# Where the last two "values" steps of a chunk put their sums, and another order of steps, in an mLSTM and GELU kernel

## The chip, the cores and the metric

One core of one Trainium2 chip runs the whole program. The metric is the time of one execution on the device, in microseconds (us); lower is better. The kernel before takes 438.91 us, the median of 3 runs from 438.79 to 439.17.

## The reference

The inputs are q, k, v and an output gate for 4 batches, 8 heads, 768 positions and 40 dimensions, an input gate and a forget gate for every position, and two weight matrices (320 x 2048 and 2048 x 320). An mLSTM cell runs over the positions; its output, seen as 3072 tokens of 320 numbers, goes through a two-layer network with exact GELU:

```
for t in range(S):
    m_new = np.maximum(f[t] + m, i[t])
    f_stab, i_stab = np.exp(f[t] + m - m_new), np.exp(i[t] - m_new)
    C = f_stab * C + i_stab * outer(v[t], k[t]);  n = f_stab * n + i_stab * k[t];  m = m_new
    y[t] = sigmoid(o[t]) * (C @ q[t]) / np.maximum(abs(n @ q[t]), 1)
h = y @ w_in                                   # 3072 x 2048
out = (0.5 * h * (1 + erf(h / sqrt(2)))) @ w_out
```

## The kernel before

**Tiles and stages.** The positions are cut into six chunks of 128. Within a chunk the recurrence is replaced by matrix products: a matrix of scores between the 128 positions (query times key), weighted by exponentials of the gates, times the values, plus the contribution of the state carried from the chunks before. A *cell* c (class `Cell`) does this for chunk c, batch by batch (b is 0 to 3). A *chunk* c (class `Chunk`) is the two-layer network on the 512 tokens that cell c made. Cell c+1 is computed while the network of chunk c runs, and its instructions are threaded between those of the network.

The network's products are made in three passes with each operand split into a high part and a rest, all on TensorE (PE in the profile). The *up* product of a chunk has four quarters. `up` (steps U0 to U3, line 966) makes a quarter's sums over the first 256 of the 320 features, in four banks of PSUM, the accumulator memory; `up_rest` (u0 to u3, line 977) adds the last 64. `gelu` (g0 to g15, lines 984 to 987) reads a bank: ScalarE (ACT) applies GELU and takes the high part, VectorE (DVE) makes the rest and the low part. `down` (d0 to d15, line 991) multiplies each of these 16 pieces with its rows of w_out and adds into four accumulators `po`, one bank each. A bank has 512 columns and `po` uses 320; the next 164 columns of each bank are called `beside`.

**The steps of a cell** inside chunks (cells 2 to 5): M masks the weight matrix W on GpSimd (POOL, line 474), W takes its exponentials (ACT, line 500), K and Q turn keys and queries (DVE, line 512), D weighs the values (POOL, line 539), S0 and S2 make the scores of two batches (PE line 568, DVE line 574), C0 and C2 read the state for two batches (`read_two`, PE line 621), h0 and h2 update it (`update_two`, PE line 632, DVE lines 639 and 647, POOL line 643), V0 to V3 multiply scores and values (`later_values`, PE line 674, DVE line 678), Y normalises and gates (`finish`, DVE lines 685 to 690), t copies the last 64 features twice (line 699), X transposes the result on PE (`turn_y`, line 708) and takes its high part on ACT (line 718), and R makes the other two parts (`split_x`, DVE lines 727 and 728). B loads the next W, J and O load the next keys, values and gates, L loads blocks of turned keys and queries, and + copies keys and queries in DRAM for later blocks, all on SyncE's DMA queue (SP). E0 to E3 copy a finished chunk's `po` out. In V0 and V1 the sums go into `beside`, in V2 and V3 into a bank of their own, which they can get only when no quarter of `up` holds it; DVE then adds the sums to `far`, the part from the state.

**Front.** Before chunk 1, cells 0 and 1 and the network of chunk 0 run in the order of the string `FRONT`. There K and J convert pieces of the weights that DMA brought as 64-bit numbers (ACT lines 404 and 405, DVE lines 416 and 419; each J fetches a later piece), A and U are quarters of `up` in plain fp32 (lines 818 and 824), u, i and f are others in split form, F are the 16 rows of `down` (line 888), z splits a piece of GELU's result (lines 873 to 875) for the last six F, and a and b make the parts of w_out (lines 935 and 943).

**What sets the order.** Every engine works through its own instructions in the order in which they are issued and waits on semaphores. The order is written out by hand in the strings: `FRONT`, then `SECOND` for chunk 1, `LATER` for chunks 2 to 4 and `LAST` for chunk 5, which has no cell beside it. A letter is a step and the number its argument. A number above 3 after M or W means the cell after the next. Inside a chunk the four banks that are not `po` are two pools of two, `side[0]` and `side[1]`; the pairs of banks of `up`, S, C and X take turns in them. Some SBUF tiles are shared by their tag in the same way: `sig` has two buffers, `o_sb` two, and a new use waits until the last reader of the old one is done.

Of the kernel before, what the change touches and what calls it, by code (L numbers as in the profile page):

```python
# [9 lines left out]
F32 = mybir.dt.float32  # L10
# [13 lines left out]


FRONT = """
    O0 L0 k1 P0 E L1 L2 t0 P1 k7 K w0 g0 N s0 w1 O1 O3 D k4 t1 P2 w2 c0 v0 J y0 Q s1 L3 O2 K d w3 q t2 L4 P3 v1
    g1 c1 J y1 s2 K x0 t3 x1 v2 g2 O4 J B4 g3 c2 y2 s3 B5 K x2 K L5 J T0 K v3 A y3 M1 x3 c3 G0 M0 H O7 O6 O5 J
    J i5 u0 L6 u1 K W0 J W1 I4 A K S0 T1 C0 J i6 V0 i7 u2 G2 K U M2 L7 S1 J G1 K U i8 W2 J i9 C1 T2 K
    M3 f2 S2 V1 Y0 T3 J Y1 C2 e W3 K K K J S3 J C3 f3 K X0 J K R0 J K J V2 K Y2 J J K  # L30
    K V3 X1 J K r F J K (0 )0 F J K F K J F X2 G3 F J K F Y3 R1 J K F p + + + + J F J a10,2 b10,2 z10 a12 b12 F X3 z11 F a13,3 b13,3 z12 F z13 [1 F B8 z14 F B9 R2 z15 F R3 B10 B11 F a8 b8 a9 b9 F"""
CELL = "MWGVYXRKQDCSht"

HI_AT = {3: ("w_out3", 0), 8: ("w_out3", 2), 4: ("w_out0", 0), 5: ("w_out0", 1), 6: ("w_out2", 0), 7: ("w_out2", 1), 9: ("f0", 0)}
# [1 line left out]
for at, first, key in ((HI_AT, 10, "h0"), (LO_AT, 10, "h1"), (HI_AT, 13, "b0"), (LO_AT, 13, "b1"), (HI_AT, 0, "b2"), (LO_AT, 0, "b3")):  # L36
    at.update((first + i, (key, i)) for i in range(3))
LATER = """
 U0 u0 E0 E1 E2 E3 K1 Q1 L2 D0 D1 C0 h0 M2 M3 g0 g1 g2 g3 +
 U1 u1 g4 d0 g5 d1 g6 d2 g7 S0 d3 K2 Q2 L3 W2 W3 G0 G1 G2 G3 +  # L40
 U2 V0 V1 u2 g8 d4 g9 K3 Q3 B4 B5 J0 J1 d5 g10 d6 g11 S2 L4 d7
 U3 u3 + M4 M5 Y0 Y1 D2 D3 K4 W4 W5 g12 t0 d8 g13 t1 d9 g14 X0 X1 R0 d10 g15 R1 C2 h2 O0 O1 d11 V2 V3 Y2 t2 B6 J2 d12 Y3 t3 Q4 L5 B7 d13 X2 X3 R2 d14 R3 d15 + O2 O3"""

SECOND = """
 U0 u0 j2 o0 o1 K1 Q1 L2 M0 M1 D0 D1 W0 W1 a0,3 b0,3 a3 b3 a4,2 b4,2 a6,2 b6,2 C0 h0 M2 M3 g0 g1 g2 g3 o2 o3 + +
 U1 u1 Z Z Z g4 d0 g5 d1 g6 d2 g7 S0 d3 K2 Q2 L3 W2 W3 G0 G1 G2 G3 Z Z +
 U2 V0 V1 u2 + g8 d4 g9 K3 Q3 B4 B5 J0 J1 d5 g10 d6 g11 S2 L4 d7
 U3 u3 + M4 M5 Y0 Y1 D2 D3 K4 W4 W5 g12 t0 d8 g13 t1 d9 g14 X0 X1 R0 d10 g15 R1 C2 h2 O0 O1 d11 V2 V3 Y2 t2 B6 J2 d12 Y3 t3 Q4 L5 B7 d13 X2 X3 R2 d14 R3 d15 + O2 O3"""

LAST = """  # L50
 U0 u0 E0 E1 E2 E3 g0 g1 g2 g3 U1 u1 g4 d0 g5 d1 g6 d2 g7 d3 
# [5 lines left out]
def kernel(  # L57
# [28 lines left out]
    TG = B * L
# [45 lines left out]
    vb = [const.tile([P, H, D1], F32, name=f"vb{n}", tag=f"vb{n}") for n in range(NQ)]  # L132
# [250 lines left out]
    bits, sig, pow2 = {}, {}, {}  # L383
# [51 lines left out]
    def per_head(t, c, b):  # L435
        return t[:, c, b * H:(b + 1) * H].unsqueeze(2)
# [21 lines left out]
    class Cell:  # L458
# [153 lines left out]
        def read_two(self, b0):  # L612

            c, two_b = self.c, (b0, b0 + 1)
            banks = self.banks = [self.side[1][0].tile([P, H + NP, D1], F32, name="pf", tag=self.side[1][1]) for _ in range(2)]
            for i, b in enumerate(two_b):
                qT = self.qT[b]
                for p in range(NP):
                    for r in halves:
                        for hip in range(2):  # L620
                            nc.tensor.matmul(banks[hip][r, NP * i + p, :], qT[halves[hip], p, r],  # L621
                                             state[b][halves[hip], p, 0:D1], start=True, stop=True)

        def update_two(self, b0):

            c, two_b, banks = self.c, (b0, b0 + 1), self.banks
            if c + 1 < NCH:
                for i, b in enumerate(two_b):
                    vw = self.vw.pop(b)
                    for p in range(NP):  # L630
                        for hip in range(2):
                            nc.tensor.matmul(banks[i][used[hip], H + p, :], k_later[turn_of(c * B + b)][:, 2 * p + hip, :],  # L632
                                             vw[:, 2 * p + hip, :], start=True, stop=True)
            add = []
            for i, b in enumerate(two_b):
                self.far[b] = fars[0].tile([P, H, D1], F32, name="far", tag="hs", bufs=2)
                by_hip = lambda t, hip: t.rearrange("p (m two) d -> p m two d", two=2)[:, :, hip, :]
                for hip in range(2):
                    nc.vector.tensor_tensor(out=by_hip(self.far[b], hip), in0=banks[hip][:, NP * i:NP * i + NP, :],  # L639
                                            in1=by_hip(per_head(gT, c - 1, b), hip).to_broadcast([P, NP, D1]), op=OP.mult)  # L640
# [19 lines left out]

        def later_values(self, b):

            n, hs = self.c * B + b, self.far.pop(b)
            Pm = W.pop(n)
            by_hip = lambda t: [t.rearrange("p (m two) d -> p m two d", two=2)[:, :, hip, :] for hip in range(2)]
            if b < 2:
                ph = beside[2 * b:2 * b + 2]
            else:
                whole = self.side[0][0].tile([P, H, D1], F32, name="ph", tag=self.side[0][1])
                ph = by_hip(whole)  # L670
            for hip in range(2):
                for p in range(NP):
                    for r in quarters:
                        nc.tensor.matmul(ph[hip][r, p, :], Pm[:, 2 * p + hip, r], vb[turn_of(n)][:, 2 * p + hip, :], start=b > 1,  # L674
                                         stop=True, skip_group_check=b < 2)
            self.hs[b] = hs
            for to, x in zip(by_hip(hs), ph) if b < 2 else ((hs, whole),):
                nc.vector.tensor_tensor(out=to, in0=x, in1=to, op=OP.add)

        def finish(self, b):  # L680
            n, hs = self.c * B + b, self.hs.pop(b)
# [18 lines left out]

        def turn_y(self, b):
            n, t = self.c * B + b, slice(b * L, (b + 1) * L)
            pool, tag = self.side[b // 2] if self.c > 1 else (ps_tr, "tr") if self.c > 0 else (ps_mm, "b")
            px = pool.tile([P, NX + 1, L], F32, name="px", tag=tag)
            unread(px[:, 0, :])
            for k in range(NX + 1):
                y = ob[n % NLD][:, k * P:(k + 1) * P] if k < NX else self.rest.get(b, y_rest).rearrange("p two r -> p (two r)")
                nc.tensor.transpose(px[:, k, :], y, ident)  # L708
            self.turned.append(b)
            if self.c < 2 and len(self.finished) > len(self.turned):  # L710
                self.twice(b + 1)
            if self.c == 0:
                nc.scalar.copy(out=first_x[:, :, t], in_=px)
                return
            self.px[b] = px
            if "x" not in parts:
                parts["x"] = raw.tile([P, NX + 1, TG], F32R, name="x_hi", tag="x", bufs=1)
            nc.scalar.activation(out=in_place(parts["x"], b), in_=by_set(px), func=AF.Copy, scale=PART)
            if self.c == 1 and b < 2:
                load(n + NLD, 1, 3)  # L720
# [12 lines left out]
    parts, fars, w_hi, w_lo, beside = {}, [], {}, {}, []  # L733
# [304 lines left out]
    def first_blocks():  # L1038
# [3 lines left out]
        for r in (32, 96):  # L1042
# [65 lines left out]
```

## Time and profile before

| | |
|---|---|
| median of 3 runs | 438.91 us |
| the profiled execution | 438.46 us |
| its span, first to last instruction | 436.7 us |
| PE busy | 427.3 us, 98% of the span |
| DVE, ACT, POOL busy | 296.0, 277.3 and 48.8 us |
| granted TensorE clock | 1.0 all through |

The profiled execution is 0.45 us under the median of the runs, and 1.8 us of it lie outside the span. The timeline view lists instructions of an engine in order of time, runs of equal ones merged: start, length, engine, line, what is written from what, the shape and, in brackets, idle time before it and what ended that. A run's length reaches to the modelled end of its last instruction, so lengths overlap the next row's start a little. The view of the chain that ended last gives pieces in order of time with start and length, without overlap, and the waits view gives who waited for whom, with total, count and longest.

### The profile page before, as it was taken

To read this page: it belongs to the slowest core of one execution; us is meant where nothing else is said; L and a number is where in the kernel's file an instruction comes from. 1 tells how busy PE (TensorE), PEld (TensorE's weight loads), DVE (VectorE), ACT (ScalarE), POOL (GpSimd) and SP (SyncE) were. 2 spreads that over 40 slices of the span, in tenths; PEclk is the share of its full clock that TensorE was granted. 3 is DMA by queue.
4 is the path that set the end of the run, shared out by engine and by line. 5 is a ranking of instruction groups with operands and counts; after the bars stand their busy time and mean duration, and the time that the engine had idled before them with its cause. 6 is when DMAs were issued, how large, how long until landed. Compare 5 with 4: busy or idle time off the path is not lost.

```text
span 436.7 us, 13291 instructions
## 1 busy us (share of the span) xinstructions
PE 427.3 (98%) x5472; PEld 374.6 (86%) x5472; DVE 296.0 (68%) x680; ACT 277.3 (63%) x595; POOL 48.8 (11%) x77
## 2 busy tenths in 40 slices
PE   8989999999999999999999999999999999999996
PEld 7777888877988899988899988899988889979986
DVE  8797687797888697747597747597746586533330
ACT  4989999856889985228785229785247715243441
POOL 3001030000430041030041030040010000000000
PEclk9999999999999999999999999999999999999999
DMA  7999994577791592662492653571561400010001
GB/s 151 220 214 243 233 256 87 138 211 179 229 154 56 106 176 60 115 179 50 84 187 42 123 158 60 117 134 32 110 156 17 62 2 2 22 42 2 1 2 60
DMA packets 162268, 48.83 MB, mean 112 GB/s; under 512 B 147776, under 2 KB 155232, under 8 KB 162208
## 3 DMA queue, kind: packets, MB, share of 16 engines
q1 hardware_dynamic: 161888, 47.65, 50.1%
q8 instruction: 43, 0.70, 0.6%
q10 hardware_dynamic: 320, 0.33, 0.2%
q14 instruction: 17, 0.14, 0.1%
HBM read 43.84 MB, written 9.37 MB: 122 GB/s over the span
## 4 chain that ended last, share of the span: by engine, by line
PE 73%; DVE 2%; ACT 2%; DMA 1%; issue 1%; ACTq 0%
PE po L991 31%; PE pu L966 24%; PE pu L977 7%; PE ps L568 3%; PE pf L621 2%; PE ph L674 1%; PE po L888 1%; PE po L674 1%; PE px L708 1%; DMA bits<-in_moe_w_out_dram 1%; PE pf L632 1%; DVE pow L416 1%; DVE w_out L419 0%; ACT w_out_part L935 0%; ACT g_part L873 0%
## 5 line engine op out<-in xcount | busy, mean ns | idle before, releaser
L991 PE MATMUL po<-w_out_part,g_parts 128*128 128x320 f32 x960 | 140.7, 303 | 0.0
L991 PEld LDWEIGHTS po<-w_out_part,g_parts 128*128 128x128 f32 x960 | 131.6, 189 | 5.9 <-issue 4.6
L986 DVE TENSOR_TENSOR g_parts<-g_whole,g_parts 128x512 fp32r<-128x512 f32 x80 | 57.0, 713 | 58.1 <-ACT g_parts L985 56.0
L984 ACT ACTIVATE g_whole<-pu 128x512 f32<-128x512 f32 x80 | 47.1, 589 | 74.2 <-PE pu L977 63.7
L985 ACT ACTIVATE g_parts<-g_whole 128x512 fp32r<-128x512 f32 x80 | 50.5, 631 | 8.3 <-PE po L991 5.1
L474 POOL TENSOR_SCALAR_AFFINE_SELECT W<-W 128x1024 f32<-128x1024 f32 (+2 forms) x20 | 21.7, 1088 | 189.2 <-DMA W<-M_d 154.4
L500 ACT ACTIVATE W<-W,aT 128x128 f32<-128x128 f32 x128 | 38.8, 389 | 0.3
L987 DVE CAST g_parts<-g_whole 128x512 fp32r<-128x512 f32 x80 | 36.2, 453 | 0.0
L699 ACT COPY far<-ob 128x128 f32<-128x128 f32 x16 | 4.6, 290 | 32.9 <-DVE ob L690 32.9
L966 PE MATMUL pu<-x_hi,w_in_hi 128*128 128x512 f32 x80 | 24.2, 384 | 0.0
L966 PE MATMUL pu<-x_hi,hi_first 128*128 128x512 f32 x80 | 24.0, 381 | 0.1
L966 PE MATMUL pu<-x_rest,hi_first 128*128 128x512 f32 x80 | 23.8, 379 | 0.0
L966 PE MATMUL pu<-x_rest,w_in_hi 128*128 128x512 f32 x80 | 23.8, 379 | 0.0
L966 PE MATMUL pu<-x_low,w_in_lo 128*128 128x512 f32 x80 | 23.8, 379 | 0.0
L966 PE MATMUL pu<-x_low,w_in 128*128 128x512 f32 x80 | 23.8, 379 | 0.0
L888 PE MATMUL po<-w_out,g 128*128 128x320 f32 x80 | 22.0, 432 | 0.0
L404 ACT ACTIVATE sig<-bits 128x320 f32<-128x320 f32 (+1 forms) x26 | 15.2, 586 | 10.4 <-issue 6.1
L574 DVE TENSOR_TENSOR W<-ps,W 128x256 f32<-128x256 f32 (+1 forms) x48 | 17.7, 414 | 4.2 <-PE ps L568 3.2
L888 PEld LDWEIGHTS po<-w_out,g 128*128 128x128 f32 x80 | 15.0, 190 | 5.9
L639 DVE TENSOR_TENSOR far<-pf,gT 128x164 f32<-128x164 f32 x32 | 8.4, 319 | 16.1 <-PE pf L632 11.7
L416 DVE SCALAR_TENSOR_TENSOR pow<-sig,pow 128x320 uint32<-128x320 uint32 (+1 forms) x26 | 15.4, 592 | 4.3 <-ACT pow L405 4.3
L1015 ACT ACTIVATE o_sb<-po 128x320 f32<-128x320 f32 x20 | 7.5, 443 | 16.7 <-PE po L991 16.7
(196 smaller groups left out, 778.9 us busy)
## 6 DMA issues: line engine op xcount, KB each, us to landing
W<-M_d SPq DMA_DIRECT2D x16, 512.0 KB, 6.5
bits<-in_moe_w_in_dram SPq DMA_DIRECT2D x20, 256.0 KB, 4.2
bits<-in_moe_w_out_dram SPq DMA_DIRECT2D x16, 320.0 KB, 4.6
blocks<-kq_d SPq DMA_DIRECT2D x32, 128.0 KB, 3.5
ob<-in_o_gate_dram SPq DMA_DIRECT2D x24, 160.0 KB, 4.1
out_dram<-o_sb SPq DMA_DIRECT2D x36, 80.0 KB, 2.0
wide<-M_d SPq DMA_DIRECT2D x4, 512.0 KB, 4.8
kq_d<-in_k_dram SPq DMA_DIRECT2D x6, 320.0 KB, 4.6
```

Of the source, the lines that this page charges most:

```text
L416: nc.vector.scalar_tensor_tensor(out=p, in0=s, scalar=3, in1=p, op0=OP.logical_shift_left, op1=OP.bitwise_or)
L474: nc.gpsimd.affine_select(out=x, in_=x, compare_op=OP.is_ge, fill=1.0e30, base=base, pattern=[[0, H], [1, x.shape[2]]], channel_multiplier=-1)
L500: nc.scalar.activation(out=W[n][:, h, :], in_=src, func=AF.Exp, scale=-1.0, bias=aT[:, self.c, r:r + 1])
L574: nc.vector.tensor_tensor(out=w[r, :, t], in0=ps[i][hip][r, :, t], in1=w[r, :, t], op=OP.mult)
L888: nc.tensor.matmul(to, xs[k][:, b * L:(b + 1) * L], w, start=(n == 0 and k == 0), stop=(n == NF - 1 and k + 1 == len(xs)), skip_group_chec ...
L966: nc.tensor.matmul(in_pairs(pus[i][e]), w3(at[k])[n][:, e, i * P:(i + 1) * P], in_turns(x3[n][:, k, :]), start=(n == 0 and k == 0), stop=F ...
L977: nc.tensor.matmul(in_pairs(pus[i][e]), w3(r)[n][h, p % 2, i * P:(i + 1) * P], in_turns(x3[n][h, NX, :]), start=False, stop=(n == 2), skip ...
L984: nc.scalar.activation(out=whole, in_=self.pus[n // 4][n % 4 // 2][n % 2], func=AF.Gelu)
L985: nc.scalar.activation(out=hi, in_=whole, func=AF.Copy, scale=PART)
L986: nc.vector.tensor_tensor(out=rest, in0=whole, in1=hi, op=OP.subtract)
L987: nc.vector.tensor_copy(out=low, in_=whole)
L991: nc.tensor.matmul(in_pairs(self.po[t]), x[:, t * L:(t + 1) * L], in_turns(w), start=(n == 0 and k == 0), stop=(n == NF - 1 and k == 2), s ...
```

## The change

Four edits belong together. V2 and V3 put their sums into the same `beside` columns as V0 and V1, without a start flag, so the columns are set to zero after V1's sums were read (four memsets). V2 and V3 no longer need `far`: DVE copies their sums into `hs`, a buffer taken from the output tiles' tag `o_sb`, and `update_two` adds `far` (for these two batches a tile of the tag `sig`) to `hs` later. C2 takes its banks from `side[0]` where it took them from `side[1]`, and X takes `side[1]` for batches 0 and 1 and `side[0]` for 2 and 3, the other way round than before. And the strings put the same steps in another order: V2 and V3 between U3 and u3, C2 and h2 ahead of X0, the four X apart, C0 between U0 and u0, M3 ahead of D0.

```diff
 FRONT = """
     ...
-    g1 c1 J y1 s2 K x0 t3 x1 v2 g2 O4 J B4 g3 c2 y2 s3 B5 K x2 K L5 J T0 K v3 A y3 M1 x3 c3 G0 M0 H O7 O6 O5 J
-    J i5 u0 L6 u1 K W0 J W1 I4 A K S0 T1 C0 J i6 V0 i7 u2 G2 K U M2 L7 S1 J G1 K U i8 W2 J i9 C1 T2 K
-    M3 f2 S2 V1 Y0 T3 J Y1 C2 e W3 K K K J S3 J C3 f3 K X0 J K R0 J K J V2 K Y2 J J K
-    K V3 X1 J K r F J K (0 )0 F J K F K J F X2 G3 F J K F Y3 R1 J K F p + + + + J F J a10,2 b10,2 z10 a12 b12 F X3 z11 F a13,3 b13,3 z12 F z13 [1 F B8 z14 F B9 R2 z15 F R3 B10 B11 F a8 b8 a9 b9 F"""
+    c1 J y1 s2 K x0 t3 x1 v2 g2 c2 O4 J B4 y2 B5 s3 g3 K L5 J T0 x2 K K M1 v3 A y3 c3 M0 G0 x3 H J O6 O5 J O7 u0
+    L6 u1 K i5 W0 J W1 A K S0 C0 I4 T1 G2 J i6 u2 U i7 V0 K M2 S1 J G1 M3 L7 K U C1 i8 J W2 T2 i9 K f2 Y0 S2 V1
+    T3 J Y1 C2 K e W3 K J K S3 J C3 f3 K X0 J K J K K R0 J K V2 Y2 J J J K K V3 (0 X1 K F G3 J )0 J
+    K F J r F J F F X2 + R1 K K p F J Y3 + F + J z10 a12 K F a10,2 b10,2 J + b12 z11 F a13,3 b13,3 z12 F F X3 z13 F
+    B8 z14 F B9 R2 z15 F [1 R3 F a8 B10 B11 a9 b9 F b8"""
 LATER = """
- U0 u0 E0 E1 E2 E3 K1 Q1 L2 D0 D1 C0 h0 M2 M3 g0 g1 g2 g3 +
- U1 u1 g4 d0 g5 d1 g6 d2 g7 S0 d3 K2 Q2 L3 W2 W3 G0 G1 G2 G3 +
- U2 V0 V1 u2 g8 d4 g9 K3 Q3 B4 B5 J0 J1 d5 g10 d6 g11 S2 L4 d7
- U3 u3 + M4 M5 Y0 Y1 D2 D3 K4 W4 W5 g12 t0 d8 g13 t1 d9 g14 X0 X1 R0 d10 g15 R1 C2 h2 O0 O1 d11 V2 V3 Y2 t2 B6 J2 d12 Y3 t3 Q4 L5 B7 d13 X2 X3 R2 d14 R3 d15 + O2 O3"""
+ E0 U0 E1 E2 K1 Q1 E3 L2 D1 C0 M3 u0 D0 h0 g0 g1 g2 g3 M2 U1 u1 g4 + d0 d1 g5 g6 d2 g7 S0 d3 K2 Q2 L3 G2 W2 W3 G3 G1 G0
+ + U2 V0 V1 u2 d4 K3 g8 Q3 B4 B5 g9 d5 J0 J1 g10 d6 g11 S2 L4 d7 U3 M5 Y0 M4 W5 W4 t0 Y1 t1 V2 V3 K4 u3 D3 D2 g12 d8 + g13
+ d9 g14 C2 h2 X0 d10 Y2 g15 X1 t2 Y3 t3 Q4 d11 R0 R1 d12 O0 O1 X2 d13 R2 B6 J2 d14 X3 R3 L5 B7 + O2 O3 d15"""
```

`SECOND` keeps its first part up to `U2 V0 V1 u2 +`; from there it becomes what `LATER` has from `d4 K3 g8` on. `LAST` stays. The code:

```diff
         def read_two(self, b0):
-            banks = self.banks = [self.side[1][0].tile([P, H + NP, D1], F32, name="pf", tag=self.side[1][1]) for _ in range(2)]
+            pool, tag = self.side[0 if b0 else 1]
+            banks = self.banks = [pool.tile([P, H + NP, D1], F32, name="pf", tag=tag) for _ in range(2)]
         def update_two(self, b0):
-                self.far[b] = fars[0].tile([P, H, D1], F32, name="far", tag="hs", bufs=2)
+                self.far[b] = (raw.tile([P, TG], F32, name="far", tag="sig")[:, 0:H * D1].rearrange("p (h d) -> p h d", d=D1) if b0 else
+                               fars[0].tile([P, H, D1], F32, name="far", tag="hs", bufs=2))
...
+            for b in two_b if b0 else ():
+                hs = self.hs[b]
+                nc.vector.tensor_tensor(out=hs, in0=self.far.pop(b), in1=hs, op=OP.add)
         def later_values(self, b):
-            n, hs = self.c * B + b, self.far.pop(b)
+            n = self.c * B + b
+            hs = self.hs[b] = self.far.pop(b) if b < 2 else outp.tile([P, 2, DM], F32, name="hs", tag="o_sb").rearrange(
+                "p two d -> p (two d)")[:, 0:H * D1].rearrange("p (h d) -> p h d", d=D1)
-            if b < 2:
-                ph = beside[2 * b:2 * b + 2]
-            else:
-                whole = self.side[0][0].tile([P, H, D1], F32, name="ph", tag=self.side[0][1])
-                ph = by_hip(whole)
+            ph = beside[b % 2 * 2:b % 2 * 2 + 2]
...
+                if b < 2:
+                    nc.vector.tensor_tensor(out=to, in0=x, in1=to, op=OP.add)
+                else:
+                    nc.vector.tensor_copy(out=to, in_=x)
+            if b == 1:
+                for x in beside:
+                    nc.vector.memset(x, 0.0)
         def turn_y(self, b):
-            pool, tag = self.side[b // 2] if self.c > 1 else (ps_tr, "tr") if self.c > 0 else (ps_mm, "b")
+            pool, tag = self.side[1 - b // 2] if self.c > 1 else (ps_tr, "tr") if self.c > 0 else (ps_mm, "b")
```

More of the change, by code (lines that the diff above doesn't have):

```diff
@@ L26 @@
 FRONT = """
-    O0 L0 k1 P0 E L1 L2 t0 P1 k7 K w0 g0 N s0 w1 O1 O3 D k4 t1 P2 w2 c0 v0 J y0 Q s1 L3 O2 K d w3 q t2 L4 P3 v1
-    g1 c1 J y1 s2 K x0 t3 x1 v2 g2 O4 J B4 g3 c2 y2 s3 B5 K x2 K L5 J T0 K v3 A y3 M1 x3 c3 G0 M0 H O7 O6 O5 J
-    J i5 u0 L6 u1 K W0 J W1 I4 A K S0 T1 C0 J i6 V0 i7 u2 G2 K U M2 L7 S1 J G1 K U i8 W2 J i9 C1 T2 K
-    M3 f2 S2 V1 Y0 T3 J Y1 C2 e W3 K K K J S3 J C3 f3 K X0 J K R0 J K J V2 K Y2 J J K
-    K V3 X1 J K r F J K (0 )0 F J K F K J F X2 G3 F J K F Y3 R1 J K F p + + + + J F J a10,2 b10,2 z10 a12 b12 F X3 z11 F a13,3 b13,3 z12 F z13 [1 F B8 z14 F B9 R2 z15 F R3 B10 B11 F a8 b8 a9 b9 F"""
+    O0 L0 k1 P0 E L1 L2 t0 P1 k7 K w0 g0 N s0 w1 O1 O3 D k4 t1 P2 w2 c0 v0 J y0 Q s1 L3 O2 K d w3 q t2 L4 P3 v1 g1
+    c1 J y1 s2 K x0 t3 x1 v2 g2 c2 O4 J B4 y2 B5 s3 g3 K L5 J T0 x2 K K M1 v3 A y3 c3 M0 G0 x3 H J O6 O5 J O7 u0
[3 more added lines that the diff above has]
+    B8 z14 F B9 R2 z15 F [1 R3 F a8 B10 B11 a9 b9 F b8"""
 CELL = "MWGVYXRKQDCSht"
@@ L38 @@
 LATER = """
- U0 u0 E0 E1 E2 E3 K1 Q1 L2 D0 D1 C0 h0 M2 M3 g0 g1 g2 g3 +
- U1 u1 g4 d0 g5 d1 g6 d2 g7 S0 d3 K2 Q2 L3 W2 W3 G0 G1 G2 G3 +
- U2 V0 V1 u2 g8 d4 g9 K3 Q3 B4 B5 J0 J1 d5 g10 d6 g11 S2 L4 d7
- U3 u3 + M4 M5 Y0 Y1 D2 D3 K4 W4 W5 g12 t0 d8 g13 t1 d9 g14 X0 X1 R0 d10 g15 R1 C2 h2 O0 O1 d11 V2 V3 Y2 t2 B6 J2 d12 Y3 t3 Q4 L5 B7 d13 X2 X3 R2 d14 R3 d15 + O2 O3"""
+ E0 U0 E1 E2 K1 Q1 E3 L2 D1 C0 M3 u0 D0 h0 g0 g1 g2 g3 M2 U1 u1 g4 + d0 d1 g5 g6 d2 g7 S0 d3 K2 Q2 L3 G2 W2 W3 G3 G1 G0
+ + U2 V0 V1 u2 d4 K3 g8 Q3 B4 B5 g9 d5 J0 J1 g10 d6 g11 S2 L4 d7 U3 M5 Y0 M4 W5 W4 t0 Y1 t1 V2 V3 K4 u3 D3 D2 g12 d8 + g13
+ d9 g14 C2 h2 X0 d10 Y2 g15 X1 t2 Y3 t3 Q4 d11 R0 R1 d12 O0 O1 X2 d13 R2 B6 J2 d14 X3 R3 L5 B7 + O2 O3 d15"""
 SECOND = """
[L45 to L48, printed above, removed]
+ U0 u0 j2 o0 o1 K1 Q1 L2 M0 M1 D0 D1 W0 W1 a0,3 b0,3 a3 b3 a4,2 b4,2 a6,2 b6,2 C0 h0 M2 M3 g0 g1 g2 g3 o2 o3 + + U1 u1 Z Z Z g4
+ d0 g5 d1 g6 d2 g7 S0 d3 K2 Q2 L3 W2 W3 G0 G1 G2 G3 Z Z + U2 V0 V1 u2 + d4 K3 g8 Q3 B4 B5 g9 d5 J0 J1 g10 d6 g11 S2 L4
+ d7 U3 M5 Y0 M4 W5 W4 t0 Y1 t1 V2 V3 K4 u3 D3 D2 g12 d8 + g13 d9 g14 C2 h2 X0 d10 Y2 g15 X1 t2 Y3 t3 Q4 d11 R0 R1 d12 O0 O1 X2
+ d13 R2 B6 J2 d14 X3 R3 L5 B7 + O2 O3 d15"""
 LAST = """
@@ L673, in later_values @@
                     for r in quarters:
[L674 to L678, printed above, removed]
+                        nc.tensor.matmul(ph[hip][r, p, :], Pm[:, 2 * p + hip, r], vb[turn_of(n)][:, 2 * p + hip, :], start=False,
+                                         stop=True, skip_group_check=True)
+            for to, x in zip(by_hip(hs), ph):
+                if b < 2:
[5 more added lines that the diff above has]
+                    nc.vector.memset(x, 0.0)
         def finish(self, b):
```

## The prediction

> **What bounds the kernel now.** First I read the page: its busy times, the engines of the chain that ended last, and the costliest groups.
>
> ```profile
> PE 427.3 (98%) x5472; PEld 374.6 (86%) x5472; DVE 296.0 (68%) x680; ACT 277.3 (63%) x595; POOL 48.8 (11%) x77
> ...
> PE 73%; DVE 2%; ACT 2%; DMA 1%; issue 1%; ACTq 0%
> ...
> L984 ACT ACTIVATE g_whole<-pu 128x512 f32<-128x512 f32 x80 | 47.1, 589 | 74.2 <-PE pu L977 63.7
> ```
>
> TensorE is busy for 98% of the span, and the chain is PE's for 73% of it. A busy PE can still lose time inside, so the second view is PE's own waits. The rows that concern steps after the first one the diff moves:
>
> ```profile
> PE pf L590 <- DVE vw L539: 0.7, 1, 0.7
> PE po L888 <- DVE g_part L874: 0.6, 2, 0.4
> ...
> PE ps L552 <- ACT qT L533: 0.4, 1, 0.4
> ```
>
> They sum to 1.7 us and all lie in the front. In the chunks PE waits for next to nothing, so there the change can win only by work or changeovers that PE no longer does, and can lose wherever it makes PE wait. The third view is therefore the chain through one chunk, chunk 2, from the pair V0 V1 to the next U0 (start, length, what):
>
> ```profile
> 213.67 1.38 PE po L674 x112
> 215.05 1.49 PE pu L977 x12
> 216.55 5.09 PE po L991 x36
> ...
> 231.63 3.46 PE po L991 x24
> 235.09 0.66 PE px L708 x6
> 235.74 1.63 PE po L991 x12
> 237.38 1.07 PE pf L621 x64
> 238.45 0.74 PE pf L632 x32
> 239.19 1.83 PE po L991 x12
> 241.02 1.51 PE ph L674 x117
> 242.53 3.46 PE po L991 x24
> 245.98 0.71 PE px L708 x6
> 246.69 3.26 PE po L991 x24
> 249.96 5.18 PE pu L966 x24
> ```
>
> Read it as PE's order: V0 V1, u2, d4 to d6; after u3, d8 d9, X0 X1, d10, C2, h2, d11, V2 V3, d12 d13, X2 X3, d14 d15, U0. Twelve matmuls of line 991 are one d: 1.63 us after X, but 1.83 after h2. A changeover from small tiles to full ones costs 0.20.
>
> **The change part by part.**
>
> *V2 and V3 between U3 and u3.* Where they stood, d11, V2 V3, d12 d13 took 1.83 + 1.51 + 3.46 = 6.80 us; three d in a row take 5.09 (x36), so taking the pair out saves 1.71. In the new place it is what V0 V1 is between U2 and u2, 1.38. That is 0.33 less per chunk. Against this the two pairs of X become four single ones, two more changeovers: at 0 to 0.20 each, and nearer 0 since d10 after X had no surcharge, I take 0.13 for both. C2 and h2 change neighbours but not number: 0. C0 between U0 and u0 trades one changeover for another: 0. Net 0.2 us per chunk, in the four chunks that have a cell beside them: 0.8 us less.
>
> *Zeroing.* Four memsets of 128x164 follow V1's sums on DVE, ahead of K3 and g8. The trace has no memset in PSUM. Bounds are 0 and the add of the same shape, whose row (with others that I use below) is in DVE's timeline:
>
> ```profile
> 214.17 1.26 DVE L678 TENSOR_TENSOR far<-po,far 128x164 f32<-128x164 f32 x4 [3.06 <-PE po L674]
> 217.22 0.69 DVE L986 TENSOR_TENSOR g_parts<-g_whole,g_parts 128x512 fp32r<-128x512 f32 x1 [1.79 <-ACT g_parts L985]
> ...
> 237.51 0.69 DVE L986 TENSOR_TENSOR g_parts<-g_whole,g_parts 128x512 fp32r<-128x512 f32 x1 [0.44 <-ACT g_parts L985]
> ...
> 239.69 1.02 DVE L639 TENSOR_TENSOR far<-pf,gT 128x164 f32<-128x164 f32 x4
> ...
> 241.98 1.10 DVE L678 TENSOR_TENSOR far<-ph,far 128x328 f32<-128x328 f32 x2
> ...
> 246.87 0.56 DVE L727 TENSOR_TENSOR x_rest<-px,x_hi 128x384 fp32r<-128x384 f32 x1 [0.27 <-ACT x_hi L718]
> ...
> 248.27 0.55 DVE L728 CAST x_low<-px 128x384 fp32r<-128x384 f32 x1
> ```
>
> Four adds took 1.26 us, so a memset is at most 0.32 and four end by 215.43 + 1.26 = 216.7 at the latest. Their cover is u2. In the old order d4 began at 216.55 with the bank that is zeroed first; the later banks follow at PE's pace, 0.14 a matmul. I take 0 and keep 0.25 per chunk as the upper end. DVE's own time is covered by the 1.79 us that it then idled until g8.
> The row alone does not say that d4 must wait, since it writes other columns of those banks. The Trainium skill, "PSUM — Partial Sum Buffer", section "PSUM bank collisions raise a hardware error", says that engines must be kept apart by bank and quadrant, not by address; by that d4 does wait for the zeroing, which is the fourth rival below, and no row here shows such a wait.
>
> *Two copies for two adds, and two adds more.* V2's and V3's sums are now copied (four of 128x164, at the adds' price 1.26), and `far` is added later (two of 128x328, at the old adds' price, 1.10). The copies have to be out before d8 writes the banks; u3's 1.49 covers them. K4 stands behind them on DVE and nobody waits for it soon. The late adds lie in the chunk's tail.
>
> *The tail's DVE work.* This is the tightest place. From the end of h2, PE now has X0, d10, X1, d11 d12, X2, d13 d14, X3, d15: four X at 0.33 (0.66 / 2) to 0.35 and six d at 1.63 are 11.1 us until U0; U0's third pair of matmuls, which reads the low part, comes 4 x 0.216 (5.18 / 24) = 0.9 later, so 12.0. In that time DVE must do what it did from 239.69 to the end of the last row, 248.82, less 0.27 idle: 8.86 us (far, states, two adds, Y2, Y3, Q4, R2, R3); plus g15 and R1, which took 237.51 to 239.69, 2.18; plus R0, at 0.56 + 0.55 about 1.1. Sum 12.1: no slack by these durations, and a few tenths if the slow second half of g15, which ran under POOL's work, comes out quicker now that POOL is idle. I take a wait of 0.1 per chunk, 0.3 us over the chunks (chunk 4 has no state to update), with 0 and 1.0 per chunk as ends.
> The Trainium skill, "SBUF — State Buffer", section "Who interferes with whom", has a rule against this part: a DVE instruction with two SBUF inputs contends with GpSimd's reads. The late adds have two SBUF inputs where the old ones had one in PSUM, and POOL scales the states just then; that would feed the first rival.
>
> *A shared buffer.* `far` of batches 2 and 3 takes the two `sig` buffers, so g15's GELU starts only after the first late add: 1.02 (far) + 0.55 = 1.57 after h2, plus 0.59 (the group on line 984) = 2.16, while X1, which needs that bank, could go after X0 and d10, 1.96. On ACT, t2 and t3 stand behind; X2 needs t2 only 3.3 later. At most 0.2 per chunk, and these lengths overlap a little; I take 0.2 us in all.
>
> *POOL and SP.* D1 and M3 now stand ahead of D0 on POOL, and h0 on PE needs D0:
>
> ```profile
> 239.12 0.73 POOL L539 TENSOR_TENSOR vw<-vb,ewT 128x328 f32<-128x328 f32 x1
> 248.00 0.73 POOL L539 TENSOR_TENSOR vw<-vb,ewT 128x328 f32<-128x328 f32 x1 [8.14 <-DMA vb<-in_v_dram]
> ...
> 259.27 1.81 POOL L474 TENSOR_SCALAR_AFFINE_SELECT wide<-wide 64x1024 f32<-64x1024 f32 x2
> ```
>
> ```profile
> 248.99 0.83 SPq L210 DMA_DIRECT2D wide<-M_d  x1
> ```
>
> ```profile
> DMA to landing us min/median/max: 4.7/4.8/8.2
> ```
>
> The first rows are old D0, old D1 and M3; the next is B7's issue, the load that M3 waits for; the last has the shortest, median and longest landing of this line's four loads. Old D0 ran at 239.12 with nothing ahead. New: B7 lands at 248.99 + 4.8 = 253.8, M3 takes 1.81, D0 0.73: 256.3. PE reaches h0 after U0, C0 and u0: 249.7 + 5.18 + 1.07 + 1.49 = 257.4. Cover 1.1 us, so 0; without it two chunks pay. On SP, O0 and O1 now wait for X1 five us later than before, with B6, J2 and L5 behind them. B6 and J2 went out at that time before, too, since they waited for V2; L5 waits for Q4 in both orders. M5 ahead of M4 and W5 ahead of W4 only swap two steps whose results are needed a chunk later: 0.
>
> *Front, z.* The last part of the front loses time between the first split F and U0:
>
> ```profile
> 107.50 0.93 PE L888 MATMUL po<-w_out_part,g_part 128*128 128x320 f32 x4
> 108.70 3.53 PE L888 MATMUL po<-w_out_part,g_part 128*128 128x320 f32 x24 [0.27 <-DVE g_part L874]
> 112.61 6.24 PE L888 MATMUL po<-w_out_part,g_part 128*128 128x320 f32 x44 [0.38 <-DVE g_part L874]
> 118.69 0.59 PE L966 MATMUL pu<-x_hi,hi_first 128*128 128x512 f32 x2
> ```
>
> From 107.50 to 118.69 are 11.19 us for 72 matmuls. The last 44 took 118.69 - 112.61 = 6.08, or 0.138 each; 72 would take 9.95. So 1.24 us are lost around the two waits for g_part. Why z was late:
>
> ```profile
> 104.68 0.50 DVE L419 SCALAR_TENSOR_TENSOR w_out<-sig,pow 128x320 uint32<-128x320 uint32 x1
> ```
>
> ```profile
> 105.26 0.50 ACT L404 ACTIVATE sig<-bits 128x320 f32<-128x320 f32 x1 [2.99 <-issue]
> ...
> 106.83 0.63 ACT L873 ACTIVATE g_part<-g 128x512 fp32r<-128x512 f32 x1
> ```
>
> ACT sat idle for 2.99 us before the last K. Its `sig` buffer was free only when J23 (DVE, to 105.18) was done, which stood behind Y3 and R1, and z10 stood behind this K. The new order has J23 ahead of Y3, and z10 and a12 ahead of the last K. z10 can then run on ACT during the idle 2.99. It needs to come 1.2 us earlier; the idle time is twice that. All 1.24 us go. What is late next is R3 for U0, and z15 with it, which is ACT's pace of about 1.2 us per z (0.63 for the high part, as much for the low one) against PE's 1.63 per F.
>
> *Front, before.* S1 waited 0.4 for turned queries; U and V0 now stand ahead of it and cover that, and U ahead of V0 covers V0's weights. c2's 0.7 goes from c2 but returns at v3, because v3 waits for DVE's scores and DVE has the same work ahead of them. I take 0.5 of the 1.1; ends 0 and 1.1. In the stretch ACT is nearly full, which is why I take no more.
>
> *Sum against the profiled execution:* -0.8 - 1.24 - 0.5 + 0.3 + 0.2 = -2.0. 438.46 - 2.0 = 436.4; the median of the runs stood 0.45 above it, so 436.9 us.
>
> **The rivals.**
> 1. *DVE becomes the bound at each chunk's end.* U0 waits for R3. The tail has no slack by the rows, so each tenth that DVE takes more is PE's. It makes the kernel slower once the wait passes 0.8 us per chunk, (2.0 + 0.3 + 0.9) / 4; at the upper end of 1.0 in four chunks, 436.9 - 0.3 + 4.0 = 440.6. For it: the sum of 12.1 against 12.0. Against: the durations I used were under POOL's load.
> 2. *h0 waits behind M3.* If B7 takes 8.2 us to land, as one load did, D0 is 8.2 - 4.8 - 1.1 = 2.3 late in two chunks: 436.9 + 4.6 = 441.5, slower; the point is a landing of 7.4. Against it: the median of 4.8.
> 3. *The front gives nothing*, because the last pieces of the weights land no earlier and J24, ahead of z10 on DVE, holds its rest back. Then 436.9 + 1.7 = 438.6, no change.
> 4. *The zeroing holds d4*, 0.25 in four chunks: 437.9, still faster.
>
> **How the numbers follow.** My forecast 0.58 (its own range 435.7 to 437.7: front ends 0 to 1.1 in place of 0.5, changeovers 0.1 to 0.3), rival 1 0.14, rival 2 0.06, rival 3 0.12, rival 4 0.10. The range for 8 in 10 reaches from 435.4, both unknown front terms at their ends, to 439.9, over rivals 3 and 4 and the milder half of rival 1. 0.2%, 0.9 us, is about what a measurement of this kernel can tell from no change. Faster by more: 0.58 + 0.10 = 0.68; within: 0.12; slower: 0.20.
>
> **What would show it.** PE's waits should no longer list L888 behind L874 nor L552 behind L533, and U0 of chunk 1 should start about 1.7 us before 118.69. From U0 to U0 a chunk should shrink by about 0.1 to 0.2 us (249.96 to the next is the ruler). V2 V3 between U3 and u3 should take about 1.4. The prediction is wrong if PE lists waits of line 966 for x_rest or x_low (rival 1), of line 632 for vw (rival 2), of line 991 for the memset (rival 4), or of line 708 for `g_whole`.

## The result and the profile after

| | before | changed |
|---|---|---|
| median of 8 runs each | 438.28 us (437.67 to 439.17) | 436.06 us (435.35 to 437.37) |
| span of the profiled execution | 436.7 us | 434.0 us |

The ratio is 0.9951, with a 95% interval from 0.9935 to 0.9966: the change makes the kernel 2.1 us faster (1.5 to 2.8). In the two profiled executions the difference is 2.7 us. One run of e6 below took 546.22 us at a granted clock of 0.753, and e6's median leaves it out.

The page of the changed kernel: busy times, and the engines of the chain that ended last.

```profile
PE 425.5 (98%) x5472; PEld 374.3 (86%) x5472; DVE 303.3 (70%) x712; ACT 279.0 (64%) x595; POOL 48.5 (11%) x77
...
PE 87%; ACT 7%; DMA 2%; SPq 1%; DVE 1%; issue 1%; ACTq 0%; DVEq 0%
```

DVE has 32 instructions and 7.3 us more, PE 1.8 us less. The second line matters most: here the shares sum to 99%, so the chain takes in the front, and 7% of it is ACT. The shares that the prediction quoted sum to 79%, so that chain stopped short of the front (its first piece starts at 85.97 us).

PE's waits in the changed kernel (who waited for whom: total, count, longest), steps of the front again:

```profile
PE ps L552 <- ACT qT L533: 0.9, 1, 0.9
...
PE pu L826 <- ACT first_x L721: 0.5, 1, 0.5
PE ph L661 <- DVE W L555: 0.2, 1, 0.2
```

The waits of c2 for weighed values (0.7) and of z's `down` for g_part (0.6) are gone. S1's wait for turned queries has grown from 0.4 to 0.9, and the other two shown are new. No wait for `x_rest`, `x_low`, `vw` or the zeroing is there.

The chain through the same stretch of chunk 2 (start, length, what), from V2 V3 to U0:

```profile
228.74 1.38 PE po L677 x115
230.12 1.49 PE pu L985 x12
231.61 3.46 PE po L999 x24
235.07 1.07 PE pf L622 x64
236.14 0.74 PE pf L633 x32
236.89 0.48 PE px L716 x3
237.36 1.63 PE po L999 x12
239.00 0.38 PE px L716 x3
239.37 3.26 PE po L999 x24
242.63 0.33 PE px L716 x3
242.96 3.26 PE po L999 x24
246.22 0.33 PE px L716 x3
246.55 1.63 PE po L999 x12
248.18 2.37 PE pu L974 x11
```

V2 V3 takes 1.38 us between U3 and u3. From d8 to U0 are 16.57 us, with V2 V3 17.95; before, 231.63 to 249.96 were 18.33. That is 0.38 less. In the timeline of PE, the distance between the first matmuls of U0 of successive chunks (us) shows how each chunk changed, here with the first two experiments beside it:

| | chunk 1 | chunk 2 | chunk 3 | chunk 4 | U0 of chunk 1 to the last `down` |
|---|---|---|---|---|---|
| before | 65.87 | 65.23 | 65.57 | 63.86 | 313.96 |
| changed | 65.04 | 64.93 | 64.87 | 63.68 | 311.95 |
| e1, old chunks, new front | 65.72 | 65.31 | 65.49 | 63.85 | 313.80 |
| e2, new chunks, old front | 65.09 | 64.95 | 64.87 | 63.61 | 311.94 |

So the chunks gave 2.0 us, and the front, up to U0 of chunk 1 (118.69 before, 118.05 now), 0.64. The end of the front in the changed kernel's timeline of PE:

```profile
107.70 2.03 PE L896 MATMUL po<-w_out_part,g_part 128*128 128x320 f32 x12
109.57 0.38 PE L716 MATMUL px<-ident,ob 128*128 128x128 f32 x2
109.79 0.27 PE L716 MATMUL px<-ident,y_rest 128*128 128x128 f32 x1
109.81 8.40 PE L896 MATMUL po<-w_out_part,g_part 128*128 128x320 f32 x60
118.05 0.59 PE L974 MATMUL pu<-x_hi,hi_first 128*128 128x512 f32 x2
```

The same 72 matmuls, without a wait and with X3 now among them, take 10.35 us in place of 11.19. X3 has left the stretch ahead, from the first split up product (62.99 before, 63.54 now) to 107.70, which takes 44.16 in place of 44.51. Together that is 1.19 gained, and 0.55 was lost ahead of 63 us.

### The profile page after: what moved, and what is told of

The parts are those of the page before. It is cut to its first block, busy times and chain, and to the rows that moved or that the text cites. A ratio compares the mean times of both kernels' runs of the same rounds, so it can differ in the third digit from the quotient of the medians.

```text
span 434.0 us, 13278 instructions
## 1 busy us (share of the span) xinstructions
PE 425.5 (98%) x5472; PEld 374.3 (86%) x5472; DVE 303.3 (70%) x712; ACT 279.0 (64%) x595; POOL 48.5 (11%) x77
## 4 chain that ended last, share of the span: by engine, by line
PE 87%; ACT 7%; DMA 2%; SPq 1%; DVE 1%; issue 1%; ACTq 0%; DVEq 0%
PE po L999 31%; PE pu L974 24%; PE po L896 7%; PE pu L985 7%; PE ps L568 3%; PE po L677 3%; PE pu L795 2%; ACT W L500 2%; PE pf L622 2%; DMA bits<-in_moe_w_in_dram 2%; PE px L716 2%; ACT pow L405 1%; PE pf L633 1%; SPq L175 1%; ACT sig L404 1%; PE pu L826 1%
## 5 line engine op out<-in xcount | busy, mean ns | idle before, releaser
L994 DVE TENSOR_TENSOR g_parts<-g_whole,g_parts 128x512 fp32r<-128x512 f32 x80 | 55.4, 692 | 50.2 <-ACT g_parts L993 47.9
L995 DVE CAST g_parts<-g_whole 128x512 fp32r<-128x512 f32 x80 | 33.9, 423 | 0.0
L726 ACT ACTIVATE x_hi<-px 128x384 fp32r<-128x384 f32 x20 | 9.8, 488 | 20.4 <-PE px L716 20.4
```

The source lines that it names most:

```text
L994: nc.vector.tensor_tensor(out=rest, in0=whole, in1=hi, op=OP.subtract)
L995: nc.vector.tensor_copy(out=low, in_=whole)
```

## The experiments

**The front alone and the chunks alone.** e1 is the kernel before with the new `FRONT`; e2 is the changed kernel with the old one.

```diff
 e1: before.   FRONT = the changed kernel's;  LATER, SECOND and the code as before
 e2: changed.  FRONT = the kernel before's;   LATER, SECOND and the code as changed
```

> The kernel before with only the new order of the front's steps; the chunks are the old ones. Theory of the two traces: the front gains 1.18 us from the first split down step on and loses 0.54 us ahead of it, so U0 of chunk 1 starts 0.64 us before 118.69 and the time is 0.6 us under the kernel before. Theory of the prediction: the front gains at both places, 1.7 us in all. If neither part of the front's gain is real: 0.

> The changed kernel with the old order of the front's steps: only the chunks' part of the change. Theory of the two traces: the chunks alone give 2.0 us (0.82, 0.32, 0.69 and 0.18 from U0 to U0), so 2.0 us under the kernel before, and U0 of chunk 1 starts at 118.7. Theory of the prediction: 0.8 less 0.5 of waits, 0.3 us under the kernel before. If a part of the 2.0 was a chance stall in the profiled execution of the kernel before (0.35 within V3 of chunk 1 and 0.26 at U3 of chunk 3 in its records), some 1.4.

Measured against the kernel before: e1 0.9972 (0.9957 to 0.9987), 1.2 us faster; e2 0.9933 (0.9915 to 0.9950), 2.9 us faster (2.2 to 3.7). The chunks are the larger part, as the traces had it and not as the prediction had it. e1's interval (0.6 to 1.9 us) holds both of its forecasts, 0.6 and 1.7. The two do not add up to the 2.1 of the whole change: that was measured beside other runs of the kernel before (median 438.28, here 439.37, later 438.8 to 438.9). So small differences between an experiment and the changed kernel are read from the traces.

The table above shows e2's chunks equal to the changed kernel's within 0.1 and e1's equal to the old ones within 0.15. Both executions with old chunks have two pauses of PE that the changed chunks do not have at these places. The first is in chunk 1: V3 stops shortly before its end, with no releaser that the profile shows. First the kernel before, then e1:

```profile
175.90 0.79 PE L674 MATMUL ph<-vb,wide 128*32 128x41 f32 x61
177.04 0.27 PE L674 MATMUL ph<-vb,wide 128*32 128x41 f32 x3 [0.35 <-issue]
```

```profile
175.78 0.79 PE L675 MATMUL ph<-vb,wide 128*32 128x41 f32 x63
176.84 0.20 PE L675 MATMUL ph<-vb,wide 128*32 128x41 f32 x1 [0.27 <-issue]
```

With it V2 V3 took 2.09 us (175.15 to 177.24) in place of 1.50 in chunk 3 (306.52 to 308.02). The changed kernel has no such stop, and with that chunk 1 gains 0.83. What makes it is open: in a later run (e7) V2 V3 of chunk 2 took 1.72 in place of 1.38 in their new place.

The second is ahead of U3 in chunk 3, which gains 0.70: d7 and U3 took 7.34 in place of the 7.00 of chunk 2 (7.28 in e1). The first bank that U3 takes holds scores of S2 until DVE has weighted them, and DVE was late. DVE, PE and POOL in the kernel before:

```profile
288.18 1.31 DVE L987 CAST g_parts<-g_whole 128x512 fp32r<-128x512 f32 x1
289.41 1.40 DVE L574 TENSOR_TENSOR W<-ps,W 128x256 f32<-128x256 f32 x4
```

```profile
290.29 0.67 PE L966 MATMUL pu<-x_hi,hi_first 128*128 128x512 f32 x2
```

```profile
288.03 1.97 POOL L474 TENSOR_SCALAR_AFFINE_SELECT W<-W 64x1024 f32<-64x1024 f32 x2 [0.65 <-DMA W<-M_d]
```

The second of the four ends at 290.15, 0.15 ahead of U3, and the same 0.15 stands in e1; elsewhere it is 0.8. The cast took 1.31 in place of 0.42 while POOL masked weights (M4, M5). In the old chunks 1 to 3 POOL began with that 2.5 to 4.6 us before U3, in the changed kernel's from 2.2 us before to 0.1 after, so that the casts were done. M5 ahead of M4 is the likely reason, but no run here tries that swap alone.

**What sets the early front.** The new order of the front's first half seemed to have lost 0.55 us. e3 takes the old order up to X1; e4 undoes one place only, x3 behind c3, with M1, M0 and G0 beside it.

```diff
 e3: FRONT = old up to V3 X1 J, then  K (0 K F G3 J )0 J K F J r ...  as changed
 e4:
-... T0 x2 K K M1 v3 A y3 c3 M0 G0 x3 H ...
+... T0 x2 K K v3 A y3 M1 x3 c3 G0 M0 H ...
```

> The changed kernel with the old order of the front's steps up to the first split down step, and the new one from there on. If the 0.54 us that the early front lost comes from the order of its steps, the first split down step starts at 85.5 as in the kernel before, U0 of chunk 1 at 117.5, and the time is 0.5 us under the changed kernel, 2.7 us under the kernel before. If the early loss is owed to something else (the later steps, or chance), no difference from the changed kernel.

> The changed kernel with one place of the front as it was: the turned outputs of batch 3 (x3) ahead of that batch's states (c3), and the scores' batch 3 (v3) ahead of the mask M1. If the first up product's wait of 0.47 us at 42.04 for ACT's copy of x3 is what the early front lost, that wait goes and 0.4 to 0.5 us are gained on the changed kernel. If the loss is made at S1 (0.92 us for the turned queries in place of 0.35), the gain at 42 is eaten there by a longer wait: 0 to 0.1.

Measured: e3 0.9928 (0.9908 to 0.9948), e4 0.9922 (0.9900 to 0.9945). These cannot be told apart, and their traces show why: the old order does not start the first split up product at one time. What moves it stands on ACT. The row where ACT goes on after its idle time at 31 us, in the kernel before, in e2 (the same front), in the changed kernel and in e4:

```profile
32.59 0.69 ACT L404 ACTIVATE sig<-bits 128x512 f32<-128x512 f32 x1 [0.96 <-DMA bits<-in_moe_w_in_dram]
```

```profile
33.78 0.70 ACT L403 ACTIVATE sig<-bits 128x512 f32<-128x512 f32 x1 [2.02 <-DMA bits<-in_moe_w_in_dram]
```

```profile
32.83 0.67 ACT L404 ACTIVATE sig<-bits 128x512 f32<-128x512 f32 x1 [1.35 <-DMA bits<-in_moe_w_in_dram]
```

```profile
33.27 0.70 ACT L404 ACTIVATE sig<-bits 128x512 f32<-128x512 f32 x1 [1.78 <-DMA bits<-in_moe_w_in_dram]
```

It waits for the fourth piece of weights, and everything behind follows (times in us):

| | piece on ACT | first split up product | distance | U0 of chunk 1 |
|---|---|---|---|---|
| before | 32.59 | 62.99 | 30.40 | 118.69 |
| e2, old order | 33.78 | 64.14 | 30.36 | 119.47 |
| e3, old order | 33.62 | 63.99 | 30.37 | 118.50 |
| changed | 32.83 | 63.54 | 30.71 | 118.05 |
| e1, new order | 33.32 | 64.00 | 30.68 | 118.56 |
| e4, new order but x3 | 33.27 | 63.64 | 30.37 | 118.16 |

The distance is 30.4 where x3 stands ahead of c3, and 30.6 to 30.8 with the new order (also in e5, e6b, e7, e8 and e10); e9 below is apart. So the new order costs 0.3 us at this one place, and the other 0.24 of the loss is the piece that landed at another time, which from one execution to the next is good for 1.7 us (32.11 in e8, 33.78 in e2). The chain of the changed kernel runs through that piece and then along ACT to S1; its first pieces and its end there:

```profile
28.89 3.84 DMA bits<-in_moe_w_in_dram
...
41.51 0.49 ACT first_x L721
...
46.24 2.23 ACT W L500 x8
...
48.60 2.43 ACT W L500 x8
...
55.16 0.49 ACT qT L533
...
55.69 1.16 PE ps L552 x16
```

PE's waits in this stretch are what ACT's chain leaves over. When e4 took the wait at 42 us away, PE waited elsewhere: 0.6 at 49.37 for DVE's weighting of S0's scores, and still 0.9 at S1. The gain is ACT's own. From the end of its GELU to the end of the conversion that reads x3's copy it took 2.66 us in the changed kernel (40.51 to 43.17), where that copy stands right ahead of the conversion, and 2.39 in e4 (40.92 to 43.31).

Next, that load: e9 issues it ahead of another one.

```diff
 e9: e4, and
-... q t2 L4 P3 v1 ...  J T0 x2 K K v3 A y3 ...
+... q t2 P3 L4 v1 ...  J x2 K K v3 A T0 y3 ...
```

> The changed kernel with x3 ahead of c3 as before, the load of the fourth piece of weights (P3) issued ahead of batch 4's queries and keys (L4) in place of behind them, and T0, which turns these, after the first up product. In six profiled executions ACT sat idle for 0.96 to 2.02 us at 31 for this piece, and the first split up product started 30.4 to 30.7 us after the piece landed (32.59 to 33.78). If that load sets the early front, it lands some 1.9 us sooner, ACT waits for it 0 to 0.2 us, the first split up product starts at 62.0 or sooner, and 1.2 to 1.8 us are gained on the changed kernel. If the chain is set elsewhere (the products' own pace, S1's turned queries): 0 to 0.3.

Measured: 0.9936 (0.9919 to 0.9952), no gain on the changed kernel. The piece came sooner (ACT took it at 31.71 without a wait), but other loads came later. DVE, then ACT:

```profile
37.47 0.50 DVE L533 TENSOR_TENSOR vw<-vb,ewT 128x328 f32<-128x328 f32 x1 [2.55 <-DMA vb<-in_v_dram]
```

```profile
47.83 2.45 ACT L494 ACTIVATE W<-W,aT 128x128 f32<-128x128 f32 x8 [1.21 <-POOL W L468]
```

The first split up product started at 65.11. So e9 moved more than the one load, and it does not test that load alone. The loads share DMA engines that are nearly full here, as the DMA view of the kernel before shows for 15 to 40 us:

```profile
DMA packets 14184, 5.58 MB, mean 223 GB/s; under 512 B 12774, under 2 KB 12803, under 8 KB 14179
...
q1 hardware_dynamic: 14179, 5.52, 97.5%
```

Nine packets in ten are under 512 bytes. The Trainium skill, "DMA: Bandwidth & Descriptors", section "Specifications", gives 512 bytes as the least for full rate; no run here tried larger packets, so whether their size sets the 223 GB/s at 97.5% is not shown.

**The slack of DVE's tail.** e5 repeats the last cast to x_low of a chunk's tail once, e6 three times (e6b is the same kernel, run once more for a profile).

```diff
+            for _ in range(2 if self.c > 1 and b == 3 else 1):      # e6, e6b: 4
+                nc.vector.tensor_copy(out=in_place(parts["x_low"], b), in_=px)
```

> The changed kernel with one more copy of 128x384 (the cast to x_low of batch 3, done twice) in DVE's tail of each of chunks 1 to 4: DVE's work there grows by 0.55 us, ahead of U0. The prediction's sum says that the tail has no slack (12.1 us of work in 12.0), so 0.55 in four chunks: 2.2 us slower than the changed kernel, at the kernel before. By the changed kernel's trace the tail takes 11.55 us and ends when U0 starts, and U0 needs it some 0.9 us later: no difference.

> The same with three more copies, 1.65 us a chunk. The prediction's sum: 1.65 in four chunks, 6.6 us slower than the changed kernel. A slack of 0.8 to 0.9: 0.75 to 0.85 in four chunks, 3.0 to 3.4 us slower than the changed kernel, and PE's waits then list U0's third pair of matmuls behind the cast of line 736.

> The kernel with three more copies of 128x384 in DVE's tail once more, for its profile. Its time was 4.9 us above that of the one with a single copy more, 1.2 us a chunk, where a slack of 0.8 to 0.9 gave 0.8. If the copies cost 0.55 each, U0's third pair of matmuls waits 0.8 us in chunk 2; if the slack is what the time says, 1.2 us, and 1.65 less 1.2 leaves a slack of 0.45. If DVE's copies are slower there than 0.55 (POOL at work beside them), the tail grows by more than 1.65 us and the slack is 0.8 after all.

Measured: e5 0.9937 (0.9919 to 0.9955) with chunks as in the changed kernel (65.04, 64.93, 64.92, 63.72): one more copy costs nothing. e6 1.0044 (1.0024 to 1.0064), 440.87 us, 4.6 above e5's 436.28, where 3.0 to 3.4 were expected. In e6b PE's waits list it:

```profile
PE pu L975 <- DVE x_low L737: 3.9, 4, 1.0
```

U0 to the last `down` grew by 4.86 over the changed kernel. The rows of the changed kernel in chunk 2 give the slack; DVE's tail from far to the last cast, then PE:

```profile
236.66 1.07 DVE L641 TENSOR_TENSOR far<-pf,gT 128x164 f32<-128x164 f32 x4
237.65 0.90 DVE L650 TENSOR_TENSOR hs<-far,hs 128x328 f32<-128x328 f32 x2
...
247.66 0.55 DVE L736 CAST x_low<-px 128x384 fp32r<-128x384 f32 x1
```

```profile
248.02 0.59 PE L974 MATMUL pu<-x_hi,w_in_hi 128*128 128x512 f32 x2
...
248.88 0.59 PE L974 MATMUL pu<-x_low,w_in_lo 128*128 128x512 f32 x2
```

The cast ends at 248.21, U0 reads its result at 248.88: 0.67, less 0.05 for the signal (in e6b the last cast ends at 251.00 and the matmul that waits for it starts at 251.05). The expectations' 0.8 to 0.9 counted from U0's start, which was too much by the overlap. Three copies took 1.77 more in e6b, and 1.77 less 0.62 is the 1.14 by which the third pair of matmuls started late there.

**The zeroing.**

```diff
-                for x in beside:
+                for x in 3 * beside:
```

> The changed kernel with the four columns zeroed three times over (twelve memsets of 0.18 us in place of four). In the changed kernel's trace they end at 214.80 in chunk 2 and d4 starts at 215.15, 0.35 us later. If d4 waits for the zeroing, it starts 0.55 us later (its first bank's last memset ends at 215.7) to 1.15 us later (all end at 216.3), and the four chunks with a cell grow by that, 2.2 to 4.6 us. If it does not wait for it, no difference.

Measured: 439.96 us in one run; U0 to the last `down` grew by 3.9. In chunk 2 of e7, DVE and PE:

```profile
215.47 2.15 DVE L686 MEMSET po<- 128x164 f32 x12
```

```profile
217.14 2.02 PE L999 MATMUL po<-w_out_part,g_parts 128*128 128x320 f32 x12 [0.60 <-DVE po L686]
```

d4 does wait: it starts right behind the ninth memset (215.47 + 9 x 0.18 = 217.09), the last on the bank that d4 writes first. In the changed kernel that bank's only memset ends at 214.25 (the row there: 214.07, 0.73 for four) and d4 starts at 215.15, so the zeroing lies 0.9 us inside its cover.

**X in pairs.**

```diff
-... h2 X0 d10 Y2 g15 X1 t2 ... O0 O1 X2 d13 R2 B6 J2 d14 X3 R3 ...
+... h2 d10 Y2 g15 X0 X1 t2 ... O0 O1 d13 X2 X3 R2 B6 J2 d14 R3 ...
```

> The changed kernel with the transposes X in pairs again (d10, X0 X1, d11, d12, d13, X2 X3, d14): two changeovers fewer in each of chunks 1 to 4, R2 and R3 some 2 us later. If the four single X cost 0.13 to 0.2 us a chunk more than two pairs, as the prediction took (0.13) and the changed kernel's trace has it (0.15), 0.5 to 0.8 us faster than the changed kernel. If d11 or U0 then waits for DVE's R3 (one matmul group of 1.63 us and the slack are all that stands behind it), no gain or a loss of up to 1 us.

Measured: 0.9930 (0.9915 to 0.9944); chunks of 65.04, 64.86, 64.93 and 63.71, in sum 258.54 against 258.52. No gain: in chunk 2 the X take 1.32 in pairs and 1.52 single, but d10 takes 1.83 behind h2 and 1.63 behind X0, the same 0.20.

**D0 ahead of M3, and the best of both.** e8 restores the order of POOL's steps in `LATER`; e11 is e4 and e8 together.

```diff
-... D1 C0 M3 u0 D0 h0 ... M2 U1
+... D0 D1 C0 u0 h0 ... M2 M3 U1
```

> The changed kernel with the later chunks' POOL steps in the order of the kernel before: D0 and D1 ahead of C0, M3 behind M2. The second rival said that h0 can wait behind M3; the changed kernel's trace has D0 end at 190.92 and h0 start at 190.97. If h0 waits there, U0 to U0 of chunks 2 and 3 shrinks, by no more than 0.1 us each; if the load of M3 came later than 4.8 us by chance, by that more. If h0 does not wait, no difference.

> The changed kernel with x3 ahead of c3 in the front and with D0 ahead of M3 in the later chunks: the two places at which the change seems to have lost time. The first split up product starts 30.4 us after the fourth piece of weights has landed in place of 30.7, and h0 waits for nothing: 0.3 to 0.5 us under the changed kernel, some 2.6 us under the kernel before.

Measured: e8 435.35 us in one run, with chunks of 65.07, 64.97, 64.97 and 63.72, none shorter than in the changed kernel. e11 0.9930 (0.9911 to 0.9950): its distance from the fourth piece to the split product is 30.39, as expected, but U0 to the last `down` is 312.21, 0.26 longer. M3 ahead of D0 costs next to nothing, so the second rival's wait did not occur, but it was near: in chunk 2 of the changed kernel D0 ended at 190.91 and h0 started at 190.97, 0.04 late by the length of u0 (1.53 in place of 1.49); in chunk 3 0.8 were left. No kernel here is shown to be faster than the changed one, whose interval overlaps those of e2 to e5 and e9 to e11.

## Why the prediction was right, and where it was wrong

The change was right: 2.0 us forecast, 2.1 measured (436.9 us forecast, 436.06 measured). The sum behind it was not. Two terms were off by more than a microsecond, in opposite directions, and that they cancelled was luck.

- *Chunks, -0.8 forecast for the work.* From d8 to U0, chunk 2 gained 0.38 against 0.2, and 0.30 as a whole. V2 V3 took 1.38 as predicted, and the four single X cost 0.15 more (1.52 in place of 1.37), near the 0.13. The step that failed is "C2 and h2 change neighbours but not number: 0": an X now follows h2, and no d pays the 0.20 that d11 paid there (1.83 in place of 1.63); 0.33 - 0.15 + 0.20 is the 0.38. Chunks 1 and 3 gained 0.93 us beyond chunk 2's 0.30. That is the size of the two pauses that the old chunks had there (0.59 in V3, 0.34 at U3), which the prediction had not looked for: it read one undisturbed chunk and multiplied by four.
- *DVE's tail, +0.3; measured 0.* The step that failed is the sum of 12.1 in 12.0. The tail took 11.55 (236.66 to 248.21) and had until 248.88; it began 0.23 before h2 ended (236.89). The eight instructions of its four R follow each other every 0.46 to 0.48 rather than at the rows' 0.55, and g15's cast took 0.42. The first rival was near all the same: 0.62 more per chunk, and every tenth beyond it would have been PE's, as e6 shows.
- *Shared buffer, +0.2.* X1 waited for `g_whole` in chunk 4 alone, where no h2 stands ahead of it: PE started X1 0.23 late there, and this chunk gained least. The sign that the prediction gave for it shows in the chain, which goes there through g15's GELU into `g_whole` (366.73) to X1 (367.38). Right in size.
- *Zeroing 0, POOL 0.* Right in size; e7 shows the zeroing's cover. POOL's cover, 1.1 by the prediction, was used up in chunk 2, so that it cost no more was luck. The rule of the Trainium skill, "PSUM — Partial Sum Buffer", section "PSUM bank collisions raise a hardware error", that decided the fourth rival held for the order of the work: d4 waits for a zeroing that touches other columns of its bank. Whether the chip would have needed that wait, no run here can show, since the program places it.
- *Front, z, -1.24.* 1.19 measured in the profiled pair. Right in mechanism: z10 starts on ACT at 100.78 in place of 106.83, and the split F wait for nothing. The size depends on the execution: from the first split up product to U0 the old order took 55.70 in the kernel before and 55.33 in e2, the new one 54.51, so against e2 the gain is 0.82.
- *Front, before, -0.5.* Wrong in sign: +0.3 at the same landing of the fourth piece, +0.55 in the profiled pair. The step that failed is "S1 waited 0.4 for turned queries; U and V0 now stand ahead of it and cover that". It treated a wait of PE as a gap to be filled with PE's work. The stretch is one chain along ACT that starts at a load, and moving PE's steps leaves it as long as it was; S1 just waited longer. That c2's wait returns at v3 was right (0.2).
- *The third rival*, a front that gives nothing, named the right suspect, the landing of weights, at the wrong end: it holds the early front, not z.

Of what was to be seen, the waits behind line 874, V2 V3 and, but for X1 in chunk 4, the absent waits in the chunks came out; the wait of S1 did not go, U0 of chunk 1 came 0.64 sooner and not 1.7, and chunks shrank by 0.18 to 0.83 and not by 0.1 to 0.2.

## What to carry to other kernels

Before a bound is read from the chain that ended last, see whether its shares sum to 100%; where it stops short, the stretch it leaves out needs a reading of its own, engine by engine. A short wait of the busiest engine can be the visible end of a long chain on another engine, and then filling it with that engine's own steps only moves the wait. And a time that agrees with the forecast says little about the terms: each half of a change run alone, with the same milestones read from every trace, separated errors here of more than a microsecond each that cancelled.

## What the runs showed of the hardware

The landing of one 256 KB load moved by 1.7 us between the twelve executions that issue it at the same place (32.11 to 33.78 on ACT). In the seven with the changed kernel's front, U0 of chunk 1 moved with it, from 117.40 to 118.56 for landings from 32.11 to 33.32.

DVE's speed depended on POOL. In the changed kernel g14's cast ran while POOL scaled the states, and g15's did not; DVE, then POOL:

```profile
236.05 0.69 DVE L995 CAST g_parts<-g_whole 128x512 fp32r<-128x512 f32 x1
...
241.87 0.42 DVE L995 CAST g_parts<-g_whole 128x512 fp32r<-128x512 f32 x1
```

```profile
235.79 1.27 POOL L645 TENSOR_TENSOR state<-state,dec 128x164 f32<-128x164 f32 x2 [7.83 <-PE pf L622]
```

The Trainium skill, "SBUF — State Buffer", section "Who interferes with whom", lists casts among the instructions that can take the port pair shared with GpSimd; these rows agree. The late adds, for which the prediction feared the other rule of that section, ran after POOL had finished in chunk 2 (237.65 against 237.06), so they do not test it. A subtraction of line 986, which also has two SBUF inputs, does; in chunk 2 of the kernel before it took 1.58 beside POOL's mask, in place of 0.65 to 0.69. DVE, then POOL:

```profile
221.44 1.58 DVE L986 TENSOR_TENSOR g_parts<-g_whole,g_parts 128x512 fp32r<-128x512 f32 x1
```

```profile
221.27 1.20 POOL L474 TENSOR_SCALAR_AFFINE_SELECT W<-W 128x1024 f32<-128x1024 f32 x1 [25.43 <-ACT g_parts L985]
```

These rows agree with that rule too.
